# Seven half-size products in place of eight in the output projection of an attention and two feed-forward layers

## The chip, the cores and the metric

One NeuronCore of a Trainium2 chip runs the whole program; the other cores do nothing. The metric is the device time of one execution in microseconds (us). TensorE is called PE below, its weight loads PEld, VectorE DVE, ScalarE ACT, GpSimd POOL and SyncE SP.

## The reference, cut to what matters

There are 896 tokens (2 batches of 448), a model width of 768 and a hidden width of 1024. Causal attention of 12 heads is followed by a gated feed-forward layer, and that by the layer that matters here (x is the output of the layer before it):

```python
h = np.maximum(x @ w_in, 0.0)                   # x 896 x 768, w_in 768 x 1024
for k in range(K):                              # K = 3 taps over the tokens of a batch
    conv_out += conv_w[k][None, None, :] * hp[:, k:k + S, :]
gate = 1.0 / (1.0 + np.exp(-conv_out))
return (h * gate @ w_out).astype(np.float32)    # w_out 1024 x 768
```

Weights arrive as float64; the result is float32.

## The kernel before, in words

**Numbers.** Each float64 weight slice is loaded raw by SP (`load`, L147) into one of two raw buffers, and made float32 in five steps a to e (`narrow`, L131): a on ACT, b to e on DVE. Every operand of a matmul is then split into a high part (`split_h`, L80, L86) and the rest (`split_l`, L88, L90), and each product is three matmuls, high by high, high by low and low by high (`mm3`, L64 to L67), that accumulate in one PSUM bank. A split costs one ACT and one DVE or POOL instruction.

**Order.** The attention part and the first products after it follow a list written out by hand (`ORDER`, L494 to L548), inside `tc.manual_schedule` (L619), which keeps PE, ACT, DVE and POOL in the order of the list. All that follows is placed by the framework's own planner, with a few instructions pinned. In both, an engine works through its instructions strictly in its own order, and an instruction that waits holds up all behind it.

**From the second layer's x on.** The loop over e (L688 to L699) makes x2, six tiles of 128 channels by 896 tokens, high and low, in the memory tags X0 to X5. The loop over f (L703 to L730) makes the eight slices of the hidden width: six chunks c of x2 times one slice of w_in, for tokens 0 to 511 and 512 to 895 (`token_mm`, L660; 2 x 6 x 3 matmuls of 512 or 384 columns), relu into `hT` (L714), the three taps (ACT L717, DVE L718 and L719), the sigmoid (ACT L722), the product with h (POOL L723), and the split into g[f], tags Y0 to Y7 (L724, L725). While this goes on, the next w_in slices and the last three w_out slices are loaded, narrowed and split.

**The w_out stage** (L732 to L753). There are 14 outputs: seven tiles of 128 tokens by two halves of 384 output columns. Each is 8 hidden slices x 3 matmuls = 24 matmuls of 384 columns (`out_mm`, L736), 336 in all. The first six run slice by slice side by side, so that the late slices of g come last; the others run one after another. ACT copies each finished bank to SBUF (L752) and SP stores it (L753), 192 KB each. Three scratch buffers `m` serve the taps and the copies; the split w_out slices lie in tag T and in tags U0 to U5.

Of the kernel before, what the change touches and what calls it, by code (L numbers as in the profile page):

```python
# [9 lines left out]
F32 = mybir.dt.float32  # L10
I32 = mybir.dt.int32
# [8 lines left out]
def kernel(  # L20
# [43 lines left out]
    def mm3(ps_out, lh, ll, rh, rl, first, last):  # L64
        nc.tensor.matmul(ps_out, lh, rh, start=first, stop=False)  # L65
        nc.tensor.matmul(ps_out, lh, rl, start=False, stop=False)  # L66
        nc.tensor.matmul(ps_out, ll, rh, start=False, stop=last)  # L67
# [79 lines left out]
    def load(w, m, name, rows, raw=None):  # L147

        if rows:
            kt, n = 1, w.shape[1]  # L150
            src = w[m * P:(m + 1) * P, :].rearrange("p (k f) -> p k f", k=1)
        else:
            kt, n = w.shape[0] // P, P
            src = w[:, m * P:(m + 1) * P].rearrange("(k p) f -> p k f", p=P)
        raw = raws.turn(f"{name}{m}raw") if raw is None else raw

        in_order(
            nc.sync.dma_start(out=raw[:, :kt * n].rearrange("p (k f) -> p k f", k=kt), in_=src)
        )
        return raw, kt * n, f"{name}{m}"  # L160

    def convert(raw, n, name, he, le, rows=False, own=()):

        c = wcs.turn(f"{name}c")
        for s in "abcde":
            narrow(s, c[:, :n], raw.bitcast(I32)[:, :2 * n])
        tiles = []
        o = 0
        while o < n:
            if own:  # L170
                t, z = own.pop(0), min(WT, n - o)
            else:
                t, z = whls.turn(f"{name}hl"), n - o
            split_h(he, t[:, 0, :z], c[:, o:o + z])
            split_l(le, t[:, 1, :z], c[:, o:o + z], t[:, 0, :z])
            tiles += [t[:, :, x:x + WT] for x in range(0, z, WT)] if rows else [t]
            o += z
        return tiles
# [18 lines left out]
    mu = const.tile([P, 4 * NC + 3 * 16], F32, name="mu")  # L197
    cw = const.tile([P, 3 * NF], F32, name="cw")

    early = [f"Y{c}" for c in range(NC)] + [f"U{e}" for e in range(3)]  # L200
# [8 lines left out]
    mixed = act.tile([P, NC, B, S], F32, tag="T", name="mixed")  # L209
    xr = [big(f"Y{c}", f"xr{c}") for c in range(NC)]  # L210
    xk = {}
    sr = {}
# [54 lines left out]
    class Job:  # L267
# [168 lines left out]
    units += [(w_v, e, "wv", False) for e in range(NE)] + [(w_in, f, "wi", False) for f in range(NF)]  # L436

    wo_after = [NE + f for f in (2, 5)] + [NE + NF + e for e in (1, 3, 5)] + [2 * NE + NF + 3] + [len(units) - 1] * 2
# [6 lines left out]
    wo, wo_slots = [], []  # L445

    small = {}

# [180 lines left out]

    def load_next():  # L630
        if plan:
            loaded.append((plan[0][3], load(*plan.pop(0))))

    def convert_next():

        if not loaded:
            load_next()
        if len(loaded) < 2:
            load_next()
        rows, x = loaded.pop(0)  # L640
        if rows:
            own = [wo_slots.pop(0) for _ in range(min(2, len(wo_slots)))]
            wo.append(convert(*x, "s", "v", True, own))
        else:
            ready.append(convert(*x, "s", "v"))
# [56 lines left out]
    g = []  # L702
    for f in range(NF):  # L703
        w = take()
        g.append(big(f"Y{f}", f"g{f}"))
        (_, lo), (_, hi) = token_mm(f"ph{f}", w, x2, f == 0)
        cut = 512 - S
        parts = [[(0, S, lo[:, :S])], [(0, cut, lo[:, S:]), (cut, S, hi)]]
        for b in range(B):
            t = TOK[b]  # L710
            hT = hp_.tile([P, S + 2], F32, tag="hT", name=f"hT{f}_{b}")
            nc.gpsimd.memset(hT[:, 0:S + 2:S + 1], 0.0)
            for z0, z1, ph in parts[b]:
# [12 lines left out]
        if f == 3:
            convert_next()
        if f == NF - 1:
            convert_next()
            convert_next()  # L730

    of = out.rearrange("b s e -> (b s) e")  # L732
    NH = WT
    outs = [(m, n) for m in range(NT // P) for n in range(2)]

    def out_mm(po, m, n, f):  # L736
        t, wt = slice(m * P, (m + 1) * P), wo[f][n]
        mm3(po, g[f][:, 0, t], g[f][:, 1, t], wt[:, 0], wt[:, 1], f == 0, f == NF - 1)

    for o0 in range(0, len(outs), 6):  # L740
        group = outs[o0:o0 + 6]
        pos = [next_bank(f"pout{m}_{n}")[:, :NH] for m, n in group]

        todo = [(f, i) for i in range(len(group)) for f in range(NF)]
        if o0 == 0:
            todo.sort()
        for f, i in todo:
            out_mm(pos[i], *group[i], f)
            if f == NF - 1:
                m, n = group[i]  # L750
                osb = mslots.turn(f"osb{m}_{n}")
                nc.scalar.activation(osb[:, :NH], pos[i], AF.Copy)  # L752
                nc.sync.dma_start(out=of[m * P:(m + 1) * P, n * NH:(n + 1) * NH], in_=osb[:, :NH])  # L753


# [31 lines left out]
```

## Time and profile before

| | us |
|---|---|
| median of 3 runs | 361.05 |
| lowest and highest of them | 359.73, 361.35 |
| the profiled execution, its own time | 359.91 |
| its span, first to last instruction | 358.1 |
| PE busy in the span | 351.9 (98%) |
| DVE busy | 280.6 (78%) |
| ACT busy | 223.8 (62%) |
| POOL busy | 96.7 (27%) |

A matmul's recorded duration overlaps the next one's, so the pace of PE is read from the starts of neighbouring matmuls and not from the durations. The same holds, less strongly, for DVE and ACT. Shares over the whole span mix stages; windows keep them apart.

### The profile page before, as it was taken

How to read it: one execution, taken by the hardware profiler on the slowest of the kernel's cores; microseconds unless marked ns; L12 is line 12 of the kernel's file. 1: busy time of each engine (PE TensorE's matmuls, PEld its weight loads, DVE VectorE, ACT ScalarE, POOL GpSimd, SP SyncE). 2: the span in 40 equal slices, each digit the busy share in tenths (PEclk: the TensorE clock that was granted, in tenths of full speed). 3: DMA queues.
4: the chain of work that ended last, by engine and by line, in shares of the span. 5: the costliest groups of instructions: out<-in, count | busy, mean ns of one | idle time of the engine just before them, and what ended most of it. 6: DMA issues, size and time to landing. Idle time of an engine off the chain costs nothing.

```text
span 358.1 us, 7189 instructions
## 1 busy us (share of the span) xinstructions
PE 351.9 (98%) x2718; PEld 316.0 (88%) x2718; DVE 280.6 (78%) x554; ACT 223.8 (62%) x482; POOL 96.7 (27%) x157
## 2 busy tenths in 40 slices
PE   7999999999999999999999999999999999999996
PEld 7678788888999998888998889999988899999995
DVE  2999999998989787888999998889999999200000
ACT  2999999999451376777786465346777757121111
POOL 3376986677534000000000000000533534200000
PEclk9999999999999999999999999999999999999999
DMA  5686577551133054545537243454215000012111
GB/s 124 149 214 138 121 193 209 127 156 49 32 116 115 14 176 167 176 150 174 192 133 228 95 150 125 166 177 134 78 56 161 15 3 0 2 66 91 65 44 45
DMA packets 60351, 41.39 MB, mean 116 GB/s; under 512 B 34424, under 2 KB 59292, under 8 KB 60316
## 3 DMA queue, kind: packets, MB, share of 16 engines
q1 hardware_dynamic: 59388, 40.70, 38.2%
q8 instruction: 21, 0.34, 0.4%
q10 hardware_dynamic: 928, 0.23, 0.3%
q14 instruction: 14, 0.11, 0.1%
HBM read 38.17 MB, written 2.75 MB: 114 GB/s over the span
## 4 chain that ended last, share of the span: by engine, by line
PE 94%; ACT 2%; DVE 2%; POOL 1%; issue 0%; POOLq 0%; ACTq 0%
PE po L391 6%; PE pk L66 5%; PE pk L67 5%; PE pout L66 5%; PE pk L65 5%; PE ph L66 5%; PE ph L67 5%; PE pout L67 5%; PE pout L65 5%; PE pv L67 5%; PE pv L66 5%; PE ph L65 5%; PE pv L65 5%; PE pr L65 5%; PE pr L66 4%; PE pr L67 4%
## 5 line engine op out<-in xcount | busy, mean ns | idle before, releaser
L723 POOL TENSOR_TENSOR cv<-cv,hT 128x448 f32<-128x448 f32 x16 | 22.9, 1436 | 170.5 <-ACT cv L722 164.8
L343 ACT ACTIVATE p<-e,st 128x448 f32<-128x448 f32 (+6 forms) x84 | 42.3, 510 | 1.7 <-DVE st L334 1.5
L71 POOL TENSOR_SCALAR p<-p,st 128x64 f32<-128x64 f32 (+6 forms) x70 | 34.6, 513 | 21.8 <-DVE st L334 12.4
L752 ACT ACTIVATE osb<-pout 128x384 f32<-128x384 f32 x14 | 6.7, 491 | 41.4 <-PE pout L67 41.4
L334 DVE CUSTOM_DVE_ANT_0 e<-s,mask 128x192 f32<-128x192 f32 (+6 forms) x84 | 31.6, 415 | 0.4 <-ACT p L343 0.2
L391 PE MATMUL po<-pt,v 128*64 128x128 f32 (+4 forms) x384 | 24.0, 277 | 0.0
L391 PEld LDWEIGHTS po<-pt,v 128*64 128x64 f32 x384 | 20.0, 137 | 3.3 <-issue 0.3
L321 PE MATMUL s<-kT,qT 64*64 64x384 f32 (+6 forms) x336 | 22.1, 387 | 0.5 <-DVE kT L78 0.2
L321 PEld LDWEIGHTS s<-kT,qT 64*64 64x64 f32 x336 | 14.9, 132 | 6.5 <-ACT qT L78 0.6
L343 ACT ACTIVATION_READ_ACCUMULATOR p<-e,st 128x1 f32 x84 | 16.6, 198 | 0.0
L66 PE MATMUL pout<-wo_t,g 128*128 128x384 f32 x49 | 16.4, 335 | 0.0
L65 PE MATMUL pout<-wo_t,g 128*128 128x384 f32 x49 | 16.4, 334 | 0.0
L67 PE MATMUL pout<-wo_t,g 128*128 128x384 f32 x49 | 16.4, 334 | 0.0
L67 PE MATMUL pout<-wo_u,g 128*128 128x384 f32 x42 | 14.0, 334 | 0.0
L65 PE MATMUL pout<-wo_u,g 128*128 128x384 f32 x42 | 14.0, 334 | 0.0
L66 PE MATMUL pout<-wo_u,g 128*128 128x384 f32 x42 | 14.0, 334 | 0.0
L719 DVE SCALAR_TENSOR_TENSOR cv<-hT,cw,cv 128x448 f32<-128x448 f32 x16 | 13.7, 857 | 0.1
L90 DVE TENSOR_TENSOR g<-cv,g 128x448 fp32r<-128x448 f32 x16 | 12.1, 757 | 1.8 <-ACT g L86 1.8
L86 ACT ACTIVATE g<-cv 128x448 fp32r<-128x448 f32 x16 | 9.2, 576 | 6.8 <-POOL cv L723 6.7
L718 DVE SCALAR_TENSOR_TENSOR cv<-hT,cw,cv 128x448 f32<-128x448 f32 x16 | 12.9, 812 | 0.0
L90 POOL TENSOR_TENSOR xr<-m,xr 128x448 fp32r<-128x448 f32 x10 | 12.0, 1196 | 2.1 <-ACT xr L86 1.7
L717 ACT ACTIVATE cv<-hT,cw 128x448 f32<-128x448 f32 x16 | 10.6, 669 | 2.3 <-DVE g L90 2.1
(524 smaller groups left out, 1230.0 us busy)
## 6 DMA issues: line engine op xcount, KB each, us to landing
rqk<-in_q_dram SPq DMA_DIRECT2D x24, 112.0 KB, 2.7
out_dram<-osb SPq DMA_DIRECT2D x14, 192.0 KB, 1.9
rqk<-in_k_dram SPq DMA_DIRECT2D x22, 112.0 KB, 3.1
v<-in_v_dram SPq DMA_DIRECT2D x24, 96.0 KB, 3.2
wv0raw<-in_moe_w_v_dram SPq DMA_DIRECT2D x1, 1024.0 KB, 6.0
wv1raw<-in_moe_w_v_dram SPq DMA_DIRECT2D x1, 1024.0 KB, 4.7
wv2raw<-in_moe_w_v_dram SPq DMA_DIRECT2D x1, 1024.0 KB, 4.9
wv3raw<-in_moe_w_v_dram SPq DMA_DIRECT2D x1, 1024.0 KB, 4.9
```

Of the source, the lines that this page charges most:

```text
L65: nc.tensor.matmul(ps_out, lh, rh, start=first, stop=False)
L66: nc.tensor.matmul(ps_out, lh, rl, start=False, stop=False)
L67: nc.tensor.matmul(ps_out, ll, rh, start=False, stop=last)
L71: nc.gpsimd.tensor_scalar(out_, in_, s, 1.0, ALU.mult, ALU.mult)
L90: e.tensor_tensor(out_, x, f32(h), ALU.subtract)
L321: nc.tensor.matmul(held[self.name(f"s{f}")][1][h, o:z], qT[r, i * LO:(i + 1) * LO], kT[r, :(i + 1) * LO], start=True, stop=True,)
L334: nc.vector.tensor_tensor_reduce(t[:, :w], used(self.name(f"s{f}"))[:, o:z], mask[:, S - w:], -SCALE, 3e38, ALU.add, ALU.min, self.st[:, 0 ...
L343: nc.scalar.activation(p[:, :w], self.s[i][:, :w], AF.Exp, bias=self.st[:, 0, i:i + 1], scale=-1.0, accum_out=self.st[:, 1, i:i + 1],)
L391: nc.tensor.matmul(self.T["po"][j * D:(j + 1) * D, 1 + i * LO - z:1 + (i + n) * LO], self.v[:, kc, j], self.T["pt"][:, a - z:a + n * LO], ...
L718: nc.vector.scalar_tensor_tensor(a, hc, cw[:, NF + f:NF + f + 1], a, ALU.mult, ALU.add)
L719: nc.vector.scalar_tensor_tensor(a, hT[:, 2:S + 2], cw[:, 2 * NF + f:2 * NF + f + 1], a, ALU.mult, ALU.add)
L723: nc.gpsimd.tensor_tensor(a, a, hc, ALU.mult)
```

## The change

The token tiles 0 to 2 (block A1) and 4 to 6 (block A2), the hidden slices 0 to 3 and 4 to 7, and the two column halves N1 and N2 cut the w_out product into 2 x 2 blocks (A11, A12, A21, A22 times B11, B12, B21, B22). Instead of eight block products it forms seven, P1 to P7, each of 3 token tiles x 4 hidden slices k x 3 matmuls = 36 matmuls, 252 in all. Token tile 3 is multiplied as before (`c0`, `c1`: 48 matmuls). The seven products need sums of blocks as operands: S1 to S4 of g and T1 to T4 of w_out, for each k, and sums of the finished products.

- On DVE it adds 20 sums of 128 x 384 (tokens `:d`), 32 low splits of them (`:l`) and 10 sums out of PSUM (`C..`). On ACT it adds 32 high splits (`:h`), 8 copies (`k`, `:c`) and the copies of product sums.
- 20 further sums are made by DMAs that POOL issues and that add to their destination (`:x`, `:y`), 192 KB each, one after another where they add to the same tile.
- The product with h of all eight slices (`m`) moves from POOL to DVE.
- The w_out slices stay narrowed as float32 in slots of the tags T and U; T1 = B12 - B11 and the split of B11 are made at their conversion.
- The split sums are kept in 12 pairs of tiles that are cut from the tags X0 to X5, two from each, handed out in the order X0, X0, X1, X1 and so on (`pair`); these tags hold x2 until then. A pair whose products are done goes to the end of the line.
- The chunks and halves of the eight w_in slices, the taps, the conversions, the sums and the w_out products all follow one list, `LATE`, on PE, ACT, DVE and POOL. `ph6l.0` is chunk 0 of hidden slice 6 for tokens 0 to 511, `P5.1.1` is product 5, token tile 1, k = 1, and `S10:h` is the high split of S1 for k = 0.

The diff, cut to its core:

```diff
+    def pair(name):
+        x = pairs.pop(0)
+        if isinstance(x, tuple):
+            e, i = x
+            if e not in st:
+                st[e] = late[0].tile([P, 2, 2, WT], F32R, tag=f"X{e}", name=f"st{e}")
+            x = st[e][:, i]
+        pair_of[name] = x
+        return x
...
+    def add_in_place(dst, x):
+        nc.gpsimd.dma_start(out=dst, in_=f32(x), accum_op=ALU.add)
...
+    def sum_step(nm, k, s):
+        x = value(nm, k)
+        v2 = nc.vector.tensor_tensor
+        if s in "hl":
+            key = f"{nm}{k}"
+            t = pair(key) if s == "h" else pair_of[key]
+            if s == "h":
+                split_h("s", t[:, 0], x)
+            else:
+                split_l("v", t[:, 1], x, t[:, 0])
...
+    pairs, pair_of, st = [(e, i) for e in range(NE) for i in range(2)], {}, {}
...
-            nc.gpsimd.tensor_tensor(a, a, hc, ALU.mult)
...
+            (nc.gpsimd if eng == "p" else nc.vector).tensor_tensor(a, a, hc, ALU.mult)
...
+        lhs, rhs = {
+            "P1": lambda: (g[k][:, :, o], operand(f"b{k}", 4)),
+            "P2": lambda: (g[KH + k][:, :, o], b2[KH + k][:, :, N1]),
+            "P3": lambda: (operand(f"S4{k}", 3)[:, :, o], b2[KH + k][:, :, N2]),
+            "P4": lambda: (g[KH + k][:, :, o2], operand(f"T4{k}", 3)),
+            "P5": lambda: (operand(f"S1{k}", 3)[:, :, o], operand(f"T1{k}", 4)),
+            "P6": lambda: (operand(f"S2{k}", 3)[:, :, o], operand(f"T2{k}", 3)),
+            "P7": lambda: (operand(f"S3{k}", 3)[:, :, o], operand(f"T3{k}", 3)),
+        }[p_]()
...
+    with tc.manual_schedule(engines={ET.PE, ET.Activation, ET.DVE, ET.Pool}):
+        for token in LATE.split():
+            issue_late(token)
```

The part of the list in which the w_in products end and the w_out products begin:

```diff
+        o5:h l4.1 ph7l.1 l3.1 ph7h.3 ph7l.2 S10:d ph7h.5 o4:l ph7l.4 m4.0/v ph6h.3 r5.1 P1.1.0 o7:e t5.1 k3 t5.0
+        h4.0 u5.1 l4.0 v5.1 S10:h T20:d g5.1 ph6h.2 c0.0 ph6l.3 r7.2 ph6h.4 S10:l T11:h m5.1/v S20:d r7.1 u5.0
+        P1.1.2 ph6l.2 ph6h.0 t7.1 S11:d v5.0 T10:h T13:h u7.1 ph6l.1 g5.0 ph6l.4 T11:l T30:h v7.1 S11:h h5.1 S11:l
+        ph6l.0 g7.1 T31:h l5.1 m5.0/v P5.1.1 h5.0 r6.2 c0.3 S20:x S21:d r6.1 T10:l m7.1/v T13:l r6.0 P1.0.0 S20:h
```

In it `r` is a relu, `t`, `u`, `v` are the three taps, `g` the sigmoid, `m` the product with h and `h`, `l` without a colon the split of g; `r`, `t`, `g`, `h` and `k` run on ACT, `u`, `v`, `m`, `l` and `:d` on DVE.

## Rows read from the trace of the kernel before

**Rows 1.** The page, part 2: busy tenths of 40 slices of the span

```profile
PE   7999999999999999999999999999999999999996
...
DVE  2999999998989787888999998889999999200000
ACT  2999999999451376777786465346777757121111
POOL 3376986677534000000000000000533534200000
```

**Rows 2.** Windows: the w_in products, then the w_out products to the last copy

```profile
238.14:296.30 58.16, 58.16 (x289) 52.21 (x289) 57.45 (x78) 39.96 (x76) 18.22 (x23) 1.00 0.25 82
296.30:354.79 58.49, 58.41 (x337) 58.09 (x336) 9.68 (x13) 14.10 (x29) 6.19 (x7) 1.00 0.12 44
```

**Rows 3.** Timeline of PE (start, duration): first w_in, first and last w_out products

```profile
238.14 0.39 PE L65 MATMUL ph<-x,wi0hl 128*128 128x512 f32 x1
238.37 0.40 PE L66 MATMUL ph<-x,wi0hl 128*128 128x512 f32 x1
...
296.30 0.33 PE L65 MATMUL pout<-wo_t,g 128*128 128x384 f32 x1
...
354.37 0.34 PE L67 MATMUL pout<-wo7hl,g 128*128 128x384 f32 x1
```

**Rows 4.** Timeline of ACT: a high split of 768, a relu of 384, the last copy

```profile
246.02 0.85 ACT L86 ACTIVATE wi4hl<-wi4c 128x768 fp32r<-128x768 f32 x1
...
302.02 0.47 ACT L714 ACTIVATE hT<-ph 128x384 f32<-128x384 f32 x1
...
354.79 0.49 ACT L752 ACTIVATE osb<-pout 128x384 f32<-128x384 f32 x1 [3.67 <-PE pout L67]
```

**Rows 5.** The page, part 6: DMA issues, KB each, us to landing

```profile
out_dram<-osb SPq DMA_DIRECT2D x14, 192.0 KB, 1.9
...
wv0raw<-in_moe_w_v_dram SPq DMA_DIRECT2D x1, 1024.0 KB, 6.0
```

**Rows 6.** Timeline of DVE: steps of 448 and 384 columns back to back

```profile
261.63 0.61 DVE L90 TENSOR_TENSOR g<-cv,g 128x448 fp32r<-128x448 f32 x1
262.17 0.68 DVE L718 SCALAR_TENSOR_TENSOR cv<-hT,cw,cv 128x448 f32<-128x448 f32 x1
262.76 0.55 DVE L141 TENSOR_SCALAR wi6c<-wi6c 128x768 int32<-128x768 int32 x1
...
286.70 0.55 DVE L90 TENSOR_TENSOR wo_u<-wo6c,wo_u 128x384 fp32r<-128x384 f32 x1
287.17 0.55 DVE L90 TENSOR_TENSOR wo6hl<-wo6c,wo6hl 128x384 fp32r<-128x384 f32 x1
```

**Rows 7.** The page, part 5: DVE and POOL groups of the taps

```profile
L723 POOL TENSOR_TENSOR cv<-cv,hT 128x448 f32<-128x448 f32 x16 | 22.9, 1436 | 170.5 <-ACT cv L722 164.8
...
L719 DVE SCALAR_TENSOR_TENSOR cv<-hT,cw,cv 128x448 f32<-128x448 f32 x16 | 13.7, 857 | 0.1
L90 DVE TENSOR_TENSOR g<-cv,g 128x448 fp32r<-128x448 f32 x16 | 12.1, 757 | 1.8 <-ACT g L86 1.8
...
L718 DVE SCALAR_TENSOR_TENSOR cv<-hT,cw,cv 128x448 f32<-128x448 f32 x16 | 12.9, 812 | 0.0
```

**Rows 8.** Timeline of DVE: the last tile of x2 is finished

```profile
243.55 0.55 DVE L90 TENSOR_TENSOR x<-xv,x 128x384 fp32r<-128x384 f32 x1
```

**Rows 9.** Windows after the last matmul (us, PE, PEld, DVE, ACT, POOL, PEclk)

```profile
355.00:356.00 1.00, 0.00 (x0) 0.00 (x0) 0.00 (x0) 0.28 (x1) 0.00 (x0) 1.00 0.00 0
356.00:357.00 1.00, 0.00 (x0) 0.00 (x0) 0.00 (x0) 0.00 (x0) 0.00 (x0) 1.00 0.55 205
357.00:358.10 1.10, 0.00 (x0) 0.00 (x0) 0.00 (x0) 0.00 (x0) 0.00 (x0) 0.64 0.00 0
```

More of the change, by code (lines that the diff above doesn't have):

```diff
@@ L62, in f32, with mm3 @@
         return ap.bitcast(F32)
[L64 to L67, printed above, removed]
+    def mm3(ps_out, lh, ll, rh, rl, first, last, more=False):
+        for i, (x, y) in enumerate(((lh, rh), (lh, rl), (ll, rh))):
+            nc.tensor.matmul(
+                ps_out, x, y, start=first and i == 0, stop=last and i == 2, skip_group_check=more,
+            )
     def scaled(eng, out_, in_, s):
@@ L160, in load, with split, convert, convert_hl @@
         return raw, kt * n, f"{name}{m}"
-    def convert(raw, n, name, he, le, rows=False, own=()):
-        c = wcs.turn(f"{name}c")
+    def split(t, x):
+        split_h("s", t[:, 0], x)
+        split_l("v", t[:, 1], x, t[:, 0])
+    def convert(raw, n, name, c=None):
+        c = wcs.turn(f"{name}c") if c is None else c
         for s in "abcde":
             narrow(s, c[:, :n], raw.bitcast(I32)[:, :2 * n])
[L167 to L178, printed above, removed]
+        return c
+    def convert_hl(raw, n, name):
+        c = convert(raw, n, name)
+        t = whls.turn(f"{name}hl")
+        split(t[:, :, :n], c[:, :n])
+        return [t]
     actx = ExitStack()
@@ L198 @@
     cw = const.tile([P, 3 * NF], F32, name="cw")
-    early = [f"Y{c}" for c in range(NC)] + [f"U{e}" for e in range(3)]
+    early = [f"T{c}" for c in range(NC)] + [f"Y{c}" for c in range(NC)] + [f"U{e}" for e in range(3)]
     late = []
@@ L207, in big @@
         return home(tag).tile([P, 2, NT], F32R, tag=tag, name=name)
-    mixed = act.tile([P, NC, B, S], F32, tag="T", name="mixed")
+    mixed = [act.tile([P, B, S], F32, tag=f"T{c}", name=f"mixed{c}") for c in range(NC)]
     xr = [big(f"Y{c}", f"xr{c}") for c in range(NC)]
@@ L435 @@
     units = [(w_r, e, "wr", False) for e in range(NE)] + [(w_k, f, "wk", False) for f in range(NF)]
-    units += [(w_v, e, "wv", False) for e in range(NE)] + [(w_in, f, "wi", False) for f in range(NF)]
-    wo_after = [NE + f for f in (2, 5)] + [NE + NF + e for e in (1, 3, 5)] + [2 * NE + NF + 3] + [len(units) - 1] * 2
+    units += [(w_v, e, "wv", False) for e in range(NE)] + [(w_in, f, "wi", False) for f in range(5)]
+    wo_after = [NE + f for f in (2, 5)] + [NE + NF + e for e in (1, 3, 5)]
     AHEAD = 2
@@ L444, with slot @@
     loaded, ready = [], []
-    wo, wo_slots = [], []
+    KH = NF // 2
+    wo_c, b11 = [], []
+    wo_slots = [f"T{c}" for c in range(NC)] + [f"U{e}" for e in range(NE)]
+    def slot(dtype, name):
+        tag = wo_slots.pop(0)
+        return home(tag).tile([P, 2, WT], dtype, tag=tag, name=name)
     small = {}
@@ L631, in load_next @@
         if plan:
-            loaded.append((plan[0][3], load(*plan.pop(0))))
+            rows = plan[0][3]
+            x = load(*plan.pop(0))
+            loaded.append((rows, x))
     def convert_next():
@@ L640, in convert_next @@
         rows, x = loaded.pop(0)
[L641 to L645, printed above, removed]
+        if not rows:
+            ready.append(convert_hl(*x))
+            return
+        i = len(wo_c)
+        if i < KH:
+            t = slot(F32R, f"b11_{i}")
+        wo_c.append(c := convert(*x, slot(F32, f"wo{i}c").rearrange("p a b -> p (a b)")))
+        if i < KH:
+            split(t, c[:, :WT])
+            nc.vector.tensor_tensor(c[:, :WT], c[:, WT:2 * WT], c[:, :WT], ALU.subtract)
+            b11.append(t)
     def take():
@@ new lines @@
+    """
+    hp_ = ctx.enter_context(tc.tile_pool(name="hp", bufs=3))
+    T3 = 3 * P
+    A1, AC, A2 = slice(0, T3), slice(T3, NT - T3), slice(NT - T3, NT)
+    N1, N2 = slice(0, WT), slice(WT, DM)
+    C0, CUT = S - T3, 512 - S
+    of = out.rearrange("b s e -> (b s) e")
+    while len(ready) < 3:
+        convert_next()
+    while len(loaded) < 2:
+        load_next()
+    w_c = {3: convert(*loaded.pop(0)[1])}
+    w_raw = {4: loaded.pop(0)[1][0]}
+    raws.held["i4"] = raws.free.pop()
+    wcs.held["i3"] = wcs.free.pop()
@@ new lines, with once @@
+    w_hl = {f: ready[f][0] for f in range(3)}
+    for f in (2, 1, 0):
+        whls.held[f"i{f}"] = whls.free.pop()
+    o_raw, b2 = {}, {}
+    wo_c.append(slot(F32, "wo5c").rearrange("p a b -> p (a b)"))
+    s1 = [x[:, i] for x in [slot(F32, f"s1_{j}") for j in range(2)] for i in range(2)]
+    hTs = Kept(hp_, "hT", 3, [P, S + 2], lambda t: [t[:, 0:S + 2:S + 1]])
+    free[:] = ring
+    g, hT, cv, left = {}, {}, {}, {}
+    def once(key, n):
+        left[key] = left.get(key, n) - 1
+        return not left[key]
@@ new lines, in first_of, with input_product @@
+    def first_of(key):
+        left[key] = left.get(key, 0) + 1
+        return left[key]
+    def input_product(f, half, c):
+        key = f"ph{f}{half}"
+        if key not in held:
+            bank(key, 2 if half == "l" else 1)
+        n, t, w = first_of("n" + key), HALF[half == "h"], w_hl[f]
+        o = slice(c * P, c * P + P)
+        mm3(
+            held[key][1][:, :t.stop - t.start], w[:, 0, o], w[:, 1, o], x2[c][:, 0, t], x2[c][:, 1, t], n == 1, n == NC,
+        )
+        if once(f"wi{f}", 2 * NC):
+            whls.put(f"i{f}")
@@ new lines, in conv_step @@
+    def conv_step(op, f, b, eng):
+        if op == "r":
+            i, b = b, min(b, 1)
+            if (f, b) not in hT:
+                hT[f, b] = hTs.get((f, b), f"hT{f}_{b}")
+            z0, z1, x0 = ((0, S, 0), (0, CUT, S), (CUT, S, 0))[i]
+            ph = used(f"ph{f}{'llh'[i]}")
+            nc.scalar.activation(hT[f, b][:, 1 + z0:1 + z1], ph[:, x0:x0 + z1 - z0], AF.Relu)
+            return
+        x = hT[f, b]
+        hc = x[:, 1:S + 1]
+        if op == "t":
+            cv[f, b] = mslots.get((f, b), f"cv{f}_{b}")[:, :S]
+        a = cv[f, b]
+        if op == "t":
+            nc.scalar.activation(a, x[:, 0:S], AF.Copy, scale=cw[:, f:f + 1])
+        elif op in "uv":
+            j = 1 + (op == "v")
@@ L728 @@
[L728 to L753, printed above, removed]
+        elif op == "m":
+            (nc.gpsimd if eng == "p" else nc.vector).tensor_tensor(a, a, hc, ALU.mult)
+            hTs.put((f, b))
+        else:
+            if f not in g:
+                g[f] = big(f"Y{f}", f"g{f}")
+            whole = b == 0 or f >= KH
+            t, a = (g[f][:, :, TOK[b]], a) if whole else (g[f][:, :, S:AC.stop], a[:, :C0])
+            if op == "h":
+                split_h("s", t[:, 0], a)
+            else:
+                split_l("v", t[:, 1], a, t[:, 0])
+            done_with(f, b)
@@ new lines, in done_with, with slice_step @@
+    def done_with(f, b):
+        if once(f"cv{f}_{b}", 2 + b):
+            mslots.put((f, b))
+    def slice_step(kind, i, s):
+        key, n, w = f"{kind}{i}", DM, w_in if kind == "i" else w_out
+        raw_, c_ = (w_raw, w_c) if kind == "i" else (o_raw, wo_c)
+        if s == "L":
+            raw_[i] = raws.get(key, f"w{key}raw")
+            load(w, i, f"w{key}", kind == "o", raw_[i])
+        elif s in "abcde":
+            if s == "a" and (kind == "i" or i > KH + 1):
+                c = wcs.get(key, f"w{key}c")
+                if kind == "i":
+                    c_[i] = c
+                else:
+                    wo_c.append(c)
+            narrow(s, c_[i][:, :n], raw_[i].bitcast(I32)[:, :2 * n])
+            if s == "e" and (kind == "i" or i < KH + 2):
+                raws.put(key)
+        else:
+            if s == "h":
+                t = whls.get(key, f"w{key}hl")[:, :, :n]
+                (w_hl if kind == "i" else b2)[i] = t
+                split_h("s", t[:, 0], c_[i][:, :n])
+            else:
+                t = (w_hl if kind == "i" else b2)[i]
+                split_l("v", t[:, 1], c_[i][:, :n], t[:, 0])
+                if kind == "i":
+                    wcs.put(key)
@@ new lines, in spare @@
+    def spare(i, j):
+        return o_raw[i].bitcast(F32)[:, j * WT:(j + 1) * WT]
+    pairs, pair_of, st = [(e, i) for e in range(NE) for i in range(2)], {}, {}
[8 more added lines that the diff above has]
+        return x
+    for k in range(KH):
+        pair_of[f"b{k}"] = b11[k]
@@ new lines, in product @@
+    def product(p_, m, k):
+        o = slice(m * P, (m + 1) * P)
+        o2 = slice(A2.start + m * P, A2.start + (m + 1) * P)
+        opens = {"P1": ("A", 4), "P5": ("B", 2), "P2": ("D", 1)}
+        n = first_of(f"{p_}.{m}")
+        if p_ in opens:
+            b_, uses = opens[p_]
+            if n == 1:
+                bank(f"{b_}{m}", uses)
+        else:
+            b_ = {"P6": "A", "P3": "B", "P7": "A", "P4": "A"}[p_]
+        lhs, rhs = {
[7 more added lines that the diff above has]
+        }[p_]()
+        mm3(
+            held[f"{b_}{m}"][1][:, :WT], lhs[:, 0], lhs[:, 1], rhs[:, 0], rhs[:, 1],
+            p_ in opens and n == 1, n == KH, p_ not in opens,
+        )
@@ new lines, in middle, with store @@
+    def middle(j, f):
+        n = first_of(f"c{j}")
+        if n == 1:
+            bank(f"c{j}", 2 - j)
+        x = g[f][:, :, AC]
+        if f >= KH:
+            y = b2[f][:, :, N2 if j else N1]
+        else:
+            y = operand(f"T1{f}" if j else f"b{f}", 4)
+        mm3(
+            held[f"c{j}"][1][:, :WT], x[:, 0], x[:, 1], y[:, 0], y[:, 1],
+            n == 1, n == NF or j == 0 and n == KH, j == 0 and n > KH,
+        )
+    def store(x, rows, cols):
+        nc.sync.dma_start(out=of[rows, cols], in_=x)
@@ new lines, in issue_late @@
+    def issue_late(token):
+        what, _, eng = token.partition("/")
+        name, _, rest = what.partition(".")
+        if what[:2] == "ph":
+            input_product(int(what[2]), what[3], int(rest))
+        elif ":" in what:
+            name, s_ = what.split(":")
+            if name[0] in "io":
+                slice_step(name[0], int(name[1]), s_)
+            else:
+                sum_step(name[:2], int(name[2]), s_)
+        elif name[0] == "P":
+            m, k = rest.split(".")
+            product(name, int(m), int(k))
+        elif name in ("c0", "c1"):
+            middle(int(name[1]), int(rest))
+        elif name[0] == "k":
+            f = int(name[1])
+            nc.scalar.activation(s1[f], cv[f, 1][:, C0:], AF.Copy)
+            done_with(f, 1)
+        elif name[0] in "cC":
+            finish(name, int(rest or 0))
+        else:
+            conv_step(name[0], int(name[1]), int(rest), eng)
```

131 lines of the change are left out of this document (103 added, 28 removed).

## The prediction

> **What bounds the kernel now.** I read the page's slices first: PE is at nine tenths or more in every slice from the second on but the last, while DVE stops six slices before the end and POOL works in the w_out stage hardly at all [rows 1]. The windows make stages of this: in the w_in products PE is busy for all of 58.16 us and DVE for 57.45, in the w_out products PE for 58.41 of 58.49 and DVE for 9.68 [rows 2]. So PE is the bound, and every matmul taken from it is time saved, as long as DVE, which has no room in the first stage and much in the second, delivers the operands in time. The pace of PE comes from starts: 0.23 us for a matmul of 512 columns, and for those of 384 columns (354.37 - 296.30) / 335 = 0.1733 us [rows 3].
>
> **The sum is made against the profiled execution**: span 358.1, own time 359.91, so 1.8 us lie around the span; that is 1.1 below the median of 361.05. I work out a difference and add it to the median. A measurement of this kernel can tell about 0.5% from no change, here 1.8 us: below 359.25 is faster, above 362.85 slower. Times below count from the first w_in product (238.14).
>
> **Fewer matmuls.** 336 become 252 + 48 = 300. 36 x 0.1733 = **-6.24 us**, and all of it counts, since PE has no pause in that stage.
>
> **DVE.** From the first w_in product it is busy 67.1 us in 91 instructions [rows 2]. Recorded durations overlap the next start by about 0.08 (0.61 and 0.54 from start to start), so 59.9 us of steps [rows 6]. The change adds 20 sums, 32 low splits and 10 sums out of PSUM, 62 steps of 384 columns at 0.47 = 29.1 [rows 6], and 16 products with h at 0.54 = 8.6. It takes away POOL's 16 instructions of 1.436 us, beside which the DVE groups of the taps and of the split took 0.857, 0.812 and 0.757 on average against 0.68, 0.68 and 0.61 undisturbed [rows 6, 7]: 16 x (0.18 + 0.13 + 0.15) = 7.3 back. That makes 59.9 + 29.1 + 8.6 - 7.3 = 90.3 us of DVE work beside 58.2 + 52.0 = 110.2 us of PE work. As a total it fits; I cost it at nothing, and PE hides it, where no single operand is late. The small sums of w_out made at conversion (one subtraction for one low split less) even out.
>
> **The start.** The last chunk of x2 is asked for by `ph0h.5`, after 7.4 us; it was finished 6.0 us after the first product, with conversion steps ahead of it on DVE that now stand behind it [rows 8]. Nothing is lost there.
>
> **The one late operand.** The list lets `S10:h` open the chain to the first P5 product, and it stands in ACT's queue before the last w_in products. But it writes the first pair of tiles, cut from X0, and X0 still holds chunk 0 of x2, which `ph6l.0` reads; that is the very last w_in product in PE's order. ACT must therefore stop at `S10:h` until `ph6l.0` has ended, and behind it in ACT's queue stand `g5.1`, `r7.2`, `T11:h`, `t7.1`, `g5.0`, `S11:h`, so that DVE, which needs them, stops at `S10:l` too. PE itself goes on: 58.16 us of w_in products and the three w_out products that are mixed in before the end (P1.1.0, c0.0, P1.1.2; 9 x 0.1733 = 1.56) bring it to 59.7. The next product, `P5.1.1`, needs `S11:l`. The way to it: the last matmul ends 0.17 us after the next could start [rows 3]; ACT starts 0.08 later, as the last copy did after the last matmul, and takes 0.49 [rows 3, 4]; then ten steps of DVE in its order, `S10:l`, `m5.1`, `S20:d`, `u5.0`, `S11:d`, `v5.0`, `u7.1`, `T11:l`, `v7.1`, `S11:l`: five of 384 columns at 0.47, four taps at 0.59 and one product at 0.54, 5.25 us [rows 6]. With three handovers of 0.08 to 0.15 that is 0.17 + 0.49 + 5.25 + 0.35 = **+6.3 us** in which PE has nothing it may do. ACT's own steps between `S10:h` and `S11:h` (ten, at 0.15 to 0.6 us) come to less than 5.25 and do not add. What stood in the shadow of the w_in products is now on the path, and the saving is spent on it.
>
> **The clock.** After the last matmul of the trace (it ends at 354.71) the granted clock is 1.00 up to 357.0 and 0.64 on average in the last 1.1 us: the lower level, 1.2 GHz, for 0.8 us of them, from 357.3 on, 2.6 us after PE fell idle [rows 3, 9]. A pause of 6.3 us is longer, so `P5.1.1` should start at half speed. How soon the clock returns no row shows. If at once, it costs nothing; if it takes as long as the pause was, 18 matmuls run where 36 would have, 3.1 us. With nothing to choose between the ends I take the middle, **+1.6 us**. The Trainium skill, page "TensorE: Matmul & The Clock Gate", Part 1, says that the half rate is the state at rest and that sustained activity has to release it; by that rule the lower end is too low and the total lies above 361.1, while with no fall of the clock it would be 361.1 and no change.
>
> **The DMAs that add.** No row shows a DMA issued by POOL or one that adds. The nearest are the store of the same 192 KB, 1.9 us to landing, and the largest load, 6.0 us [rows 5]; I take 4, between them, as it reads both its source and its destination. The first, `S20:x`, is issued within PE's pause, at 61.6, when DVE has made `S20:d`. ACT asks for its result behind the relus of slice 6 (`r6.0`), at about 66.5, so up to 5 us are covered; PE then has P1, P5, c0 and c1 products in hand, which cover one more. The Trainium skill, page "DMA: Bandwidth & Descriptors", section on the SWDGE path, gives a fixed 2.0 us plus the bytes over 436 GB/s, an estimate of 2.5 us here; by it too the sum keeps 0 for these DMAs.
>
> **The end.** The last product is followed by the same copy of 0.49 and store of 1.9 [rows 4, 5]. Three more stores are issued in the 4 us before it, where there was one in 4.2. Between 0 and 1.9 us (a whole store in front), I take **+0.2**, as a store alone is through in half the time that lies between two of them.
>
> **Sum**: -6.24 + 6.3 + 1.6 + 0.2 = +1.9, or 359.9 to 361.8 against the profiled execution and **362.9 us** against the median. With the two ends of the clock it is 361.3 to 364.5.
>
> **Rivals.** *No wait* (the faster side): if `S10:h` need not wait for X0, because its pair does not lie where x2 does, P5.1.1 depends on DVE's queue alone. DVE's steps up to `S11:l` come to 53.6 us. It loses time early: `i4:h` needs a buffer that slice 0 holds until its last chunk, at 8.0, and takes 0.85 [rows 4], so `i4:l` starts at 9.0 with only 3.15 us of DVE work done, 5.9 lost; a few steps that follow on their own result add about 1. `S11:l` ends at 60.6, and PE waits 1.0 us, too little for the clock. That gives 361.05 - 6.24 + 1.0 + 0.2 = **356.0**. For it speaks that everything else in the list lies close together without pauses; against it, that both tiles carry the tag X0 in a pool with one buffer. It decides from a wait below 4.2 us. *The clock holds*: 6.3 us of wait alone, 361.3. *The adding DMAs are slow*: above 6 us each further microsecond is paid again at `S20:h`, `S21:h`, `S23:h` and `S22:h`, which stand in ACT's one queue before relus and copies that free banks; at 8 us that is some 4 x 2 = 8 more, **371**.
>
> **How the numbers follow.** The wait with a loss of clock 0.52, of which 0.30 above and 0.22 below the bound of 362.85, as the ends 361.3 and 364.5 lie on both sides of it; the wait with the clock held 0.08; no wait 0.25; slow DMAs or a further late operand 0.15. So faster 0.25, no change 0.22 + 0.08 = 0.30, slower 0.30 + 0.15 = 0.45. The range takes in the no-wait case with half a microsecond below it and the upper end of the clock with one above it, 355.5 to 365.5; left out are the slow DMAs and little else. The likeliest case alone has 361.3 to 364.5.
>
> **What would show it.** In the profile after: 300 matmuls of 384 columns in the w_out products; ACT idle before `S10:h` for several microseconds, released by a product of line `ph`; DVE idle at `S10:l` with it; one pause of PE of about 6.3 us before the first P5 product and no other above 1; a granted clock of 0.5 behind that pause; POOL without TENSOR_TENSOR; DVE at 0.68 for the taps. A pause of PE below 4 us, or several pauses behind waits for DMAs, would prove the forecast wrong.

## The result, and the profile after

The changed kernel takes **362.47 us** (median of 6 runs, 362.12 to 364.38) beside 360.48 for the kernel before (6 runs, 359.73 to 361.35): a ratio of 1.0063, 95% interval 1.0036 to 1.0091. That is slower by a little over the half per cent that counts here, though the interval reaches below it; the forecast was 362.9, with slower as the likeliest case. One run of e7 below took 1186.61 us, three times as long as all others, and is left out of its median.

First the page of the changed kernel, parts 1 and 2, for [rows 1]:

```profile
PE 348.0 (97%) x2682; PEld 311.3 (86%) x2682; DVE 307.1 (85%) x629; ACT 234.7 (65%) x515; POOL 89.9 (25%) x148
...
PE   8899999999999999999999999999999994999995
...
DVE  1999999998989788889989988885999957997830
```

PE had 2718 matmuls and has 2682: the 36 are gone. In their place one slice, the 34th of 40, has PE at four tenths; before, it was at nine everywhere there. DVE now works nearly to the end. From the first w_in product on, the list of PE's waits (engine and line, what it waited for: us in total, times, longest) has a single row:

```profile
PE B L66 <- ACT st L87: 5.3, 1, 5.3
```

Behind it, on the timeline of PE, stands what the wait did to the pace (start, duration; in brackets the idle time before):

```profile
238.72 1.08 PE L66 MATMUL ph0l<-x,wi0hl 128*128 128x512 f32 x4
...
296.77 2.24 PE L66 MATMUL ph6l<-x,wi6hl 128*128 128x512 f32 x9
304.32 1.38 PE L66 MATMUL B<-st,st 128*128 128x384 f32 x3 [5.30 <-ACT st L87]
305.50 1.16 PE L66 MATMUL c<-b,g 128*128 128x384 f32 x3
306.46 1.16 PE L66 MATMUL A<-b,g 128*128 128x384 f32 x3
307.42 0.84 PE L66 MATMUL B<-st,st 128*128 128x384 f32 x3
308.09 0.68 PE L66 MATMUL c<-b,g 128*128 128x384 f32 x3
308.61 0.68 PE L66 MATMUL B<-st,st 128*128 128x384 f32 x3
...
355.93 0.69 PE L66 MATMUL A<-b,g 128*128 128x384 f32 x3
```

B is the bank of `P5.1.1`. From there three matmuls take 0.96 us from start to start (305.50 to 306.46) and not 0.52 (308.09 to 308.61). The windows around it, with the granted clock behind DVE's, ACT's and POOL's busy time, as in [rows 9]:

```profile
303.00:304.00 1.00, 0.00 (x0) 0.00 (x0) 1.00 (x3) 1.00 (x3) 0.00 (x0) 1.00 0.75 132
304.00:305.00 1.00, 0.68 (x2) 0.50 (x2) 1.00 (x3) 1.00 (x3) 0.00 (x0) 0.66 0.39 65
305.00:306.00 1.00, 1.00 (x5) 0.99 (x4) 1.00 (x3) 0.61 (x2) 0.00 (x0) 0.50 0.00 0
...
307.00:308.00 1.00, 1.00 (x5) 1.00 (x5) 1.00 (x3) 1.00 (x5) 0.67 (x1) 0.64 0.00 0
```

0.50 is the lower level, 1.2 GHz. Last, who let PE wait. ACT's and DVE's timelines at that place:

```profile
299.05 0.52 ACT L87 ACTIVATE st<-s 128x384 fp32r<-128x384 f32 x1 [7.62 <-PE ph6l L66]
...
302.86 0.58 ACT L811 ACTIVATE cv<-cv 128x448 f32<-128x448 f32 x1 [0.39 <-DVE cv L807]
...
303.76 0.51 ACT L87 ACTIVATE st<-s 128x384 fp32r<-128x384 f32 x1
```

```profile
299.61 0.56 DVE L91 TENSOR_TENSOR st<-s,st 128x384 fp32r<-128x384 f32 x1 [6.06 <-ACT st L87]
...
302.15 1.27 DVE L807 SCALAR_TENSOR_TENSOR cv<-hT,cw,cv 128x448 f32<-128x448 f32 x2
...
304.41 0.55 DVE L91 TENSOR_TENSOR st<-s,st 128x384 fp32r<-128x384 f32 x1
```

ACT stands for 7.62 us before `S10:h` (299.05), which writes into X0, until the last product that reads chunk 0 of x2 has ended; DVE stands for 6.06 at `S10:l` behind it. Then the chain runs: DVE to `v5.0`, the first of the two taps of 302.15, ACT's sigmoid `g5.0` at 302.86, which needs it, `T30:h`, and `S11:h`, the high part of the operand that PE is waiting for, done at 304.27.

**Where the time went.** A measure that leaves the attention part and the last stores out is the time from the start of the first w_in product to the start of the last matmul, read from PE's timeline in each trace: 116.23 us before (238.14 to 354.37), 117.56 after (238.72 to 356.28, the third matmul of the last row above). The difference of +1.33 is made of -6.24 for the matmuls, +5.46 for the pause (the last w_in matmul starts at 298.63, so the next could have started at 298.86; it did at 304.32), +1.69 for the pace behind it (15 steps from 304.32 to 308.61 take 4.29 instead of 2.60), and +0.4 in the w_in products, whose pace is a little lower. Beyond that measure the first w_in product came 0.6 later in this execution (in the traces below it comes anywhere from 237.83 to 239.31), and the tail is 0.3 longer.

### The profile page after: what moved, and what is told of

It reads as the page before. It is cut to its first block, busy times and chain, and to the rows that moved or that the text cites. A ratio compares the mean times of both kernels' runs of the same rounds, so it can differ in the third digit from the quotient of the medians.

```text
span 360.3 us, 7188 instructions
## 1 busy us (share of the span) xinstructions
PE 348.0 (97%) x2682; PEld 311.3 (86%) x2682; DVE 307.1 (85%) x629; ACT 234.7 (65%) x515; POOL 89.9 (25%) x148
## 4 chain that ended last, share of the span: by engine, by line
PE 92%; DVE 3%; DMA 1%; ACT 1%; POOL 1%; issue 1%; SPq 1%; POOLq 0%
PE pk L66 16%; PE pv L66 16%; PE pr L66 13%; PE A L66 7%; PE po L391 6%; PE s L321 4%; PE B L66 4%; PE c L66 2%; PE D L66 2%; PE W L561 2%; PE Xa L363 1%; PE q L300 1%; PE Yb L363 1%; PE ph6l L66 1%; PE ph7l L66 1%; PE ph3l L66 1%
## 5 line engine op out<-in xcount | busy, mean ns | idle before, releaser
L887 POOL DMA_DIRECT2D s<-g x12 | 12.3, 1189 | 204.5 <-DVE cv L807 190.2
L807 DVE SCALAR_TENSOR_TENSOR cv<-hT,cw,cv 128x448 f32<-128x448 f32 x32 | 21.2, 677 | 0.0
L66 PE MATMUL B<-st,st 128*128 128x384 f32 x36 | 8.7, 360 | 5.3 <-ACT st L87 5.3
L87 ACT ACTIVATE x<-xv 128x512 fp32r<-128x512 f32 (+1 forms) x12 | 6.8, 574 | 10.4 <-DVE xv L706 10.4
L811 ACT ACTIVATE cv<-cv 128x448 f32<-128x448 f32 x16 | 9.1, 572 | 6.3 <-DVE cv L807 6.2
L66 PEld LDWEIGHTS B<-st,st 128*128 128x128 f32 x36 | 6.9, 205 | 5.9 <-ACT st L87 5.7
L91 DVE TENSOR_TENSOR k<-a,k 128x512 fp32r<-128x512 f32 (+2 forms) x16 | 9.9, 618 | 0.0
L66 PE MATMUL pv<-k,wv0hl 128*128 128x512 f32 (+1 forms) x48 | 9.9, 364 | 0.0
L813 DVE TENSOR_TENSOR cv<-cv,hT 128x448 f32<-128x448 f32 x16 | 9.9, 616 | 0.0
L66 PE MATMUL pv<-k,wv5hl 128*128 128x512 f32 (+1 forms) x48 | 9.8, 363 | 0.0
```

The lines of the kernel that those rows point to most:

```text
L66: nc.tensor.matmul(ps_out, x, y, start=first and i == 0, stop=last and i == 2, skip_group_check=more,)
L807: nc.vector.scalar_tensor_tensor(a, x[:, j:S + j], cw[:, j * NF + f:j * NF + f + 1], a, ALU.mult, ALU.add)
L813: (nc.gpsimd if eng == "p" else nc.vector).tensor_tensor(a, a, hc, ALU.mult)
L887: nc.gpsimd.dma_start(out=dst, in_=f32(x), accum_op=ALU.add)
```

## The experiments

The theory: the pause exists because `S10`'s pair is cut from X0, the chunk that PE reads last; it costs its length and the clock behind it; nothing else in the list is late. Rivals: DVE is too full whatever the pair is, or the pause hides other waits. The first four runs are made from the changed kernel. The kernel before, run again beside each group, has medians of 360.55 (e1 to e4) and 360.31 (e5 to e8), so times of different groups compare to a few tenths.

**e1, the pairs in the order in which chunks fall free**

```diff
-    pairs, pair_of, st = [(e, i) for e in range(NE) for i in range(2)], {}, {}
+    pairs, pair_of, st = [(e, i) for e in (5, 3, 2, 1, 4, 0) for i in range(2)], {}, {}
```

> The pairs of tiles for the sums are handed out in the order in which the chunks of x2 fall free (5, 3, 2, 1, 4, 0) and not from 0 up; nothing else is changed. Theory (S10:h waits only because its pair lies in X0): ACT's stop of 7.6 us goes, PE's pause of 5.3 us before P5.1.1 shrinks to 1 us or less, the granted clock stays at 1.00 behind it, and the time is 362.5 - 5.3 - 1.7 + up to 1.0 = 355.5 to 356.5, clearly below the kernel before. Rival one (DVE's queue is too full for the chain, whatever the pair): the pause stays above 3 us and the time above 359.5. Rival two (the pause hides another wait, of the adding DMAs or of the banks): it turns up a few microseconds later, 358 to 360.

Measured: **355.01 us** (5 runs), ratio to the kernel before 0.9826 (0.9799 to 0.9853). PE's timeline and the window of the same place:

```profile
237.83 1.55 PE L66 MATMUL ph0l<-x,wi0hl 128*128 128x512 f32 x6
...
295.89 2.24 PE L66 MATMUL ph6l<-x,wi6hl 128*128 128x512 f32 x9
297.96 0.69 PE L66 MATMUL B<-st,st 128*128 128x384 f32 x3
298.49 0.70 PE L66 MATMUL c<-b,g 128*128 128x384 f32 x3
...
347.91 0.69 PE L66 MATMUL A<-b,g 128*128 128x384 f32 x3
```

```profile
298.00:299.00 1.00, 1.00 (x7) 1.00 (x6) 1.00 (x3) 0.58 (x2) 0.00 (x0) 1.00 0.00 0
```

`P5.1.1` follows the w_in products with no idle time at all, and PE waits for nothing from there to its last matmul. From first w_in product to last matmul it is 110.43 us, 7.13 less than in the changed kernel; pause and pace together were 5.46 + 1.69 = 7.15. Both rivals fall: one line, which only says where operands lie, holds the whole loss. This version beats both kernels.

**e2, the same wait shortened from the other side**

```diff
-        o5:h l4.1 ph7l.1 l3.1 ph7h.3 ph7l.2 S10:d ph7h.5 o4:l ph7l.4 m4.0/v ph6h.3 r5.1 P1.1.0 o7:e t5.1 k3 t5.0
-        h4.0 u5.1 l4.0 v5.1 S10:h T20:d g5.1 ph6h.2 c0.0 ph6l.3 r7.2 ph6h.4 S10:l T11:h m5.1/v S20:d r7.1 u5.0
-        P1.1.2 ph6l.2 ph6h.0 t7.1 S11:d v5.0 T10:h T13:h u7.1 ph6l.1 g5.0 ph6l.4 T11:l T30:h v7.1 S11:h h5.1 S11:l
-        ph6l.0 g7.1 T31:h l5.1 m5.0/v P5.1.1 h5.0 r6.2 c0.3 S20:x S21:d r6.1 T10:l m7.1/v T13:l r6.0 P1.0.0 S20:h
+        o5:h l4.1 ph7l.1 l3.1 ph7h.3 ph7l.2 S10:d ph7h.5 o4:l ph7l.4 m4.0/v ph6h.0 r5.1 P1.1.0 o7:e t5.1 k3 t5.0
+        h4.0 u5.1 l4.0 v5.1 S10:h T20:d g5.1 ph6h.2 c0.0 ph6l.0 r7.2 ph6h.4 S10:l T11:h m5.1/v S20:d r7.1 u5.0
+        P1.1.2 ph6l.1 ph6h.3 t7.1 S11:d v5.0 T10:h T13:h u7.1 ph6l.2 g5.0 ph6l.4 T11:l T30:h v7.1 S11:h h5.1 S11:l
+        ph6l.3 g7.1 T31:h l5.1 m5.0/v P5.1.1 h5.0 r6.2 c0.3 S20:x S21:d r6.1 T10:l m7.1/v T13:l r6.0 P1.0.0 S20:h
```

> The pairs stay as they are; of the last w_in products, those on chunks 0 and 3 change places and those on 1 and 2, so that chunk 0 is read 4.3 us before the end of the w_in products instead of last. The amount of work is the same. Theory (the wait for X0): S10:h starts 4.3 us earlier, at about 294.7, the same chain of 5.3 us follows, PE's pause is about 1.0 us, the clock holds, 362.5 - 4.3 - 1.7 = 356.5. Rival (ACT and DVE are late for a reason of their own): pause and time as in the changed kernel, 362 or more.

Measured: 356.41 us (6 runs), ratio 0.9884 (0.9851 to 0.9916). ACT's first split of the sums, and then PE:

```profile
294.41 0.52 ACT L87 ACTIVATE st<-s 128x384 fp32r<-128x384 f32 x1 [3.25 <-PE ph6l L66]
```

```profile
299.68 1.13 PE L66 MATMUL B<-st,st 128*128 128x384 f32 x3 [0.94 <-ACT st L87]
```

ACT still stops, for 3.25 us now, and the same chain follows (294.41 to 299.68); PE waits 0.94. That is the dose that was asked for, by an edit that doesn't touch the pairs.

**e3, only the first pair moved**

```diff
+    pairs.insert(0, pairs.pop())
```

> Only the last pair of the list (in X5) is put first, so that S10 is free to go and T11, the second to ask, lies in X0 and stops ACT instead. Theory: DVE does its steps up to v5.0 in the shade, and from the end of ph6l.0 on only ACT's steps from T11:h to S11:h remain, nine at 0.15 to 0.57 us, about 3.4 us: pause 3.5 us instead of 5.3. If the clock falls behind a pause of that length as well and costs the same, the time is 362.5 - 1.8 = 360.7; if it holds, 359.0. Rival (the pair is not the cause): 362 or more.

Measured: 360.5 us (12 runs), ratio 0.9998 (0.9974 to 1.0021).

```profile
303.15 1.33 PE L66 MATMUL B<-st,st 128*128 128x384 f32 x3 [3.54 <-ACT st L87]
304.28 1.17 PE L66 MATMUL c<-b,g 128*128 128x384 f32 x3
305.24 1.15 PE L66 MATMUL A<-b,g 128*128 128x384 f32 x3
306.20 0.71 PE L66 MATMUL B<-st,st 128*128 128x384 f32 x3
```

The pause is 3.54 as forecast, and the clock falls behind it all the same: three matmuls again take 0.96 (304.28 to 305.24). A pause two thirds as long costs nearly the same on top: 9 steps from 303.15 to 306.20 take 3.05 instead of 1.56, 1.49 more.

**e4, the pause filled with work that counts for nothing**

```diff
+                if p_ == "P5" and m == 1:
+                    for _ in range(26):
+                        nc.tensor.matmul(held["B1"][1][:, :WT], g[0][:, 0, o], b11[0][:, 0], start=True, stop=True)
```

> The order and the pairs stay; 26 matmuls of 384 columns on operands that are there (g0, b11) fill 4.5 us of the pause before P5.1.1, in the bank that P5.1.1 then opens anew. They end before the operand comes, so the wait itself is as long as it was. Theory (the pause costs a second time, because behind it 12 matmuls or so run at half the clock): clock 1.00 behind the pause, 362.5 - 1.7 = 360.8. Rival (what runs at half the clock is hidden by later waits of PE for DVE anyway, or the filler is late itself): 362.5 or more.

Measured: 361.19 us (12 runs), ratio 1.001 (0.9993 to 1.0027), 1.3 below the changed kernel by the medians.

```profile
299.19 4.70 PE L928 MATMUL B<-b,g 128*128 128x384 f32 x26
304.66 1.14 PE L66 MATMUL B<-st,st 128*128 128x384 f32 x3 [0.78 <-ACT st L87]
305.63 0.70 PE L66 MATMUL c<-b,g 128*128 128x384 f32 x3
```

With the operand as late as before, the matmuls behind it run at full pace. From first w_in product to last matmul it is 116.41, so 1.15 of the 1.69 come back. The rest was for the most part not the clock: `P5.1.1` also needs the low part, `S11:l`, which DVE finishes 0.7 us after `S11:h` in the changed kernel (304.96 beside 304.27); here that wait shows openly, as 0.97 us from the first matmul of `P5.1.1` to the next product instead of 0.52.

The other four are made from e1, where PE has no waits that could hide a cost.

**e5, the adding DMAs replaced by DVE**

```diff
-        nc.gpsimd.dma_start(out=dst, in_=f32(x), accum_op=ALU.add)
+        nc.vector.tensor_tensor(dst, dst, f32(x), ALU.add)
```

> On top of the order of pairs of e1 (355.0): the 20 DMAs that add become 20 additions on DVE, in the same places of the list. DVE gets 20 x 0.47 = 9.4 us more, 102.2 beside 110.4 of PE. Theory (the DMAs cost nothing where they are, and DVE, which in e1 runs without a pause from 5 us after the first w_in product to the last sums, has no room in the middle): operands of the second half come up to 9 us later, PE's lead takes part of it, 357 to 360. Rival (the totals decide, as the prediction argued for DVE): 102.2 is below 110.4, 355 to 356.

Measured: 360.93 us (12 runs), ratio 1.0011 (0.9999 to 1.0023), 5.9 above e1. DVE's busy time from the first w_in product on (the figure with 187 instructions), then PE's two longest waits of five:

```profile
238.98:359.20 120.22, 113.04 (x589) 103.88 (x588) 102.75 (x187) 68.78 (x143) 0.00 (x0) 1.00 0.19 63
```

```profile
PE A L66 <- DVE st L91: 1.3, 1, 1.3
PE D L66 <- DVE wo7raw L975: 0.8, 1, 0.8
...
```

102.8 us of DVE stand beside 110.4 of PE, so by the totals it fits, and still PE waits in five places, 3.8 us by the list. By the starts it is more, 116.51 us from first w_in product to last matmul beside 110.43: a recorded wait begins only at the recorded end of the matmul before it, 0.17 us after the next could have started, and the shortest stops are not listed. The loss is a little above the 357 to 360 of the theory. The total does not decide. That each sum's place in the list does is the likely reading; no run moved the sums to other places.

**e6, each adding DMA in two halves**

```diff
+        for z in (slice(0, WT // 2), slice(WT // 2, WT)):
+            nc.gpsimd.dma_start(out=dst[:, z], in_=f32(x[:, z]), accum_op=ALU.add)
```

> On top of e1: each DMA that adds is issued as two of half the columns, 40 instead of 20, so POOL's queue issues twice as often (0.84 to 1.05 us each, 34 to 40 us of issue in a stretch of 33) and each sum lands 1 to 3 us later. Theory (PE has enough products in hand to cover them, and the cover is several microseconds): 355 to 356, with ACT waiting for some of the sums. Rival (they were just in time): ACT's queue stops at S20:h and the like, PE pauses, 358 or more.

Measured: 361.42 us (6 runs), ratio 1.0037 (1.0023 to 1.005), 6.4 above e1. The DMA rows (KB each, median us to landing), of the changed kernel and then of this one:

```profile
s<-g POOLq DMA_DIRECT2D x12, 192.0 KB, 4.0
wo6raw<-g POOLq DMA_DIRECT2D x8, 192.0 KB, 4.8
```

```profile
s<-g POOLq DMA_DIRECT2D x24, 96.0 KB, 5.8
wo6raw<-g POOLq DMA_DIRECT2D x16, 96.0 KB, 6.0
```

Half the bytes land later (in e1 the two groups take 4.0 and 5.0). POOL, whose busy time in e1 is 12.1 us from 310 to 335, is here busy for all of these 25 us, so the issues queue up there; how much of the delay is that, and how much the transfers themselves, was not separated. ACT now waits for sums, PE behind it. Its longest such wait, then PE's timeline and a window near the end:

```profile
336.54 0.53 ACT L87 ACTIVATE b<-s 128x384 fp32r<-128x384 f32 x1 [3.62 <-DMA s<-g]
```

```profile
339.94 0.44 PE L66 MATMUL B<-wo7hl,st 128*128 128x384 f32 x1 [0.58 <-DVE st L91]
341.76 1.80 PE L66 MATMUL A<-st,st 128*128 128x384 f32 x6 [1.38 <-ACT st L87]
343.37 1.16 PE L66 MATMUL B<-wo7hl,st 128*128 128x384 f32 x3
```

```profile
343.00:344.00 1.00, 1.00 (x4) 0.99 (x4) 0.40 (x1) 0.00 (x0) 0.00 (x0) 0.50 0.00 0
```

My expectation was wrong here and its rival right: the cover is there for DMAs of 4 to 5 us and gone at 6 with a second issue on top. PE's waits come to 3.5 us, and the clock falls once more near the end.

**e7, the products with h back on POOL**

```diff
-            (nc.gpsimd if eng == "p" else nc.vector).tensor_tensor(a, a, hc, ALU.mult)
+            nc.gpsimd.tensor_tensor(a, a, hc, ALU.mult)
```

> On top of e1: the 16 products with h go back to POOL. DVE loses 16 x 0.54 = 8.6 us, but if POOL's work beside it is what made the taps slow before (0.86 and 0.81 us against 0.68 now), it gets back 16 x (0.18 + 0.14 + 0.16) = 7.7 and more on the conversions. Theory (moving the products to DVE cost DVE nothing): taps back above 0.75 us, DVE's busy time within 3 us of 92.8, time 355 to 357. Rival (the taps became faster for another reason): taps stay at 0.68, DVE's busy time falls by 8 us.

Measured: 360.07 us (median of 11 runs), ratio 1.0001 (0.9988 to 1.0014), 5.1 above e1. DVE's groups of the taps, in the changed kernel and in this one, with one conversion:

```profile
L807 DVE SCALAR_TENSOR_TENSOR cv<-hT,cw,cv 128x448 f32<-128x448 f32 x32 | 21.2, 677 | 0.0
```

```profile
L807 DVE SCALAR_TENSOR_TENSOR cv<-hT,cw,cv 128x448 f32<-128x448 f32 x32 | 25.5, 813 | 0.0
...
L144 DVE SCALAR_TENSOR_TENSOR wo6c<-wo6raw,wo6c 128x768 int32<-128x768 int32 x1 | 1.7, 1737 | 0.0
```

From the first w_in product on DVE is busy for 95.9 us with 150 instructions, where e1 has 93.0 with 166: it has less to do and takes longer. Moving the products to DVE therefore cost it less than nothing. The time was misjudged: with later products of h PE waits for both parts of `P5.1.1`'s operand, and for 0.8 us once more at a later product:

```profile
300.93 0.61 PE L66 MATMUL B<-st,st 128*128 128x384 f32 x2 [2.01 <-ACT st L87]
302.35 0.44 PE L66 MATMUL B<-st,st 128*128 128x384 f32 x1 [0.81 <-DVE st L91]
```

**e8, 36 matmuls put back**

```diff
+        for _ in range(4 if p_ in opens and n == 1 else 0):
+            nc.tensor.matmul(held[f"{b_}{m}"][1][:, :WT], lhs[:, 0], rhs[:, 0], start=True, stop=True)
```

> On top of e1: each of the nine banks that a product of P1, P5 or P2 opens first gets 4 more matmuls of 384 columns with the same operands, 36 in all, as many as the change takes away; the output stays the same. Theory (PE is the bound throughout the w_out stage once the pause is gone): 36 x 0.1733 = 6.24 more, 355.0 + 6.2 = 361.2, or 0.7 above the kernel before. Rival (DVE is so close behind that some of the matmuls fall into waits): 357 to 360.

Measured: 361.28 us (12 runs), ratio 1.0025 (1.0014 to 1.0036). The first w_in product and the last row of PE's timeline:

```profile
238.52 1.78 PE L66 MATMUL ph0l<-x,wi0hl 128*128 128x512 f32 x7
...
354.84 0.68 PE L66 MATMUL A<-b,g 128*128 128x384 f32 x3
```

By the medians that is 6.27 above e1, and from first w_in product to last matmul 116.67 beside 110.43, **6.24**: 36 x 0.1733 to the hundredth. PE waits for nothing here either. The saving of the change is real and entire; it was spent in the pause.

## Why the prediction was right

The mechanism came out as forecast; that the total came so close was in part luck. From the first w_in product on the forecast is +1.9 and the trace +1.6, because errors of opposite sign meet: the pause was taken 0.8 too long, and a loss of 0.4 in the w_in products was not foreseen.

**Fewer matmuls**, -6.24: e8 gives the same figure.

**The one late operand**, +6.3: the place, the cause and the order of the chain were right, the size 0.8 too large (5.46). The step that failed is "the next product, `P5.1.1`, needs `S11:l`". That was the mis-sized term: the first of its three matmuls is high by high and needs `S11:h` alone, which ACT had ready 0.7 us before DVE had `S11:l`. "ACT's own steps come to less than 5.25 and do not add" was also too simple: they do sum to less, but the sigmoid `g5.0` stands among them and waits for DVE's `v5.0`, so that the chain runs through both engines.

**The clock**, +1.6, taken as the middle of 0 and 3.1: 1.69 by the pace, of which e4 gives 1.15 back and the wait for `S11:l` holds most of the rest. The middle was taken for want of any row that could choose, so that it came within 0.1 is luck. Behind the pause the half rate lasted for some ten matmuls, which the trace of before could not show. The Trainium skill's rule in "TensorE: Matmul & The Clock Gate", Part 1, that activity must first release the half rate, put the total above 361.1; the rows with three matmuls in 0.96 us agree. (The 361.1 leaves out the +0.2 of the end; with it the sum without a loss of clock is the 361.3 that stands beside it.)

**DVE**, 90.3 us in total: 92.8 measured (the window of the changed kernel from 238.72), but by two errors that nearly cancel. The 67.1 of [rows 2] was busy time already free of overlap, and "59.9 us of steps" took the overlap off a second time. And the relief was larger than 7.3: 67.1 + 29.1 + 8.6 - 92.8 = 12.0 (some 2 of it because 74 instructions came on top and not 78), since conversions with two inputs also run at 0.95 us where POOL's products stretch them to 1.74 (e7). The argument around it, that a total which fits costs nothing "where no single operand is late", was the weak one: e5 has a total that fits as well and loses 5.9 us. In e1 DVE has no pause to spare in the first w_out products (1.00 in the window of 298 to 299), and the change costs nothing there because the list has each operand in time, not because there is room.

The Trainium skill's page "SBUF — State Buffer", "Who interferes with whom", says that a DVE instruction with two SBUF inputs and a POOL instruction that reads SBUF shut each other out. The taps, the low splits of g and the conversion step above have two inputs each and are stretched in e7, while the conversion steps with one input stay at 0.55 to 0.56 us, so the trace agrees.

**The DMAs that add**, 0 us at an estimated 4: 4.0 and 4.8 measured, no wait of PE or ACT for one of them in the changed kernel or in e1. The bound named, "above 6 us", is about where e6 begins to pay. The page "DMA: Bandwidth & Descriptors" of the Trainium skill, in its section on the SWDGE path, led to an estimate of 2.5 us; the trace differs by 1.5 to 2.3, and the trace decides.

**The start and the end**, 0 and +0.2: the tail is 0.3 longer. Not foreseen was the pace of the w_in products: from first w_in product to the start of `P5.1.1` e1 has 297.96 - 237.83 = 60.13 us, less nine matmuls at 0.1733 it is 58.57 beside 58.16 of [rows 2]. The list mixes slices and halves, but whether that costs these 0.4 us was not tried.

**The rival *No wait*** at 356.0 is e1, at 355.0: it is what the change gives once the first pairs lie in chunks of x2 that have been read to the end. Its 1.0 us of wait for DVE did not come about; DVE stood for 3.7 us at `i4:l` in e1, where 5.9 had been reckoned as lost.

## What to carry to other kernels

When operands are written into memory that an earlier stage frees, hand the places out in the order in which that stage falls silent; a list that is right in every dependency still stops an in-order engine at the first write that comes too soon, and all behind it moves from the shade onto the path. Price such a stop by what the queue has to do after it, through all engines, and add the slower pace of TensorE that may follow it. And don't trust a total that fits: move the work once, and see who waits.

## What the runs showed that was not expected

**The length of a pause does not tell what it costs.** In the profiled run of e7 PE stood still for 2.01 us before `P5.1.1` and for 0.81 more within it, and the clock stayed at 1.00. In that of e6 it stood for 0.58 and then 1.38, less in all, and the granted clock was 0.50 from 343 to 346, though PE had been at work again since 341.76; three matmuls took 0.95 us there (343.37 to 344.32). A pause of 3.54 (e3) cost about as much pace as one of 5.30. An estimate by length alone, as the prediction's bounds for the clock, is no more than that.

**Nor does the kernel alone decide it.** The mean granted clock of a whole run of e7 is 1.00 in five runs and 0.990 to 0.995 in six; in e6 it is 0.999 in three and 0.995 in three. All runs of the changed kernel and of e3 have 0.989 to 0.994. In e7 the runs with the lower clock are not the slower ones: 359.24 to 360.91 us beside 360.04 to 361.22. Where in these runs the clock fell, no trace shows, so the 1.69 us above are the price in one profiled execution.

**POOL's issue of a DMA is work.** An adding DMA that is issued alone holds POOL for 0.84 to 1.05 us, and cutting each in two was worse: e6 moves the same bytes, POOL's busy time rises from 17.4 us in e1 to 35.2, and each half lands 1.0 to 1.8 us later than the whole did.
